# W_down in one run of 36 rows a partition, its operand turned on VectorE: a change at the end of a transfer-bound decode kernel

## The chip, the cores and the metric

The kernel runs on one core of one Trainium2 chip. The metric is device microseconds of one execution; lower is better. Executions are repeated, and medians are given with their range. A profiled execution gives the trace; its span, from the first to the last instruction, is about 1.3 us shorter than the time.

## The reference, cut to what matters

One decode step for four sequences: attention over the last 4,096 cached positions of 16 key and value heads, a residual, a layer norm, then a gated feed-forward block and a second residual. The change touches only the last matrix product and what feeds it.

```python
h  = x + attention(layernorm(x), k_cache, v_cache, wq, wo)      # cut
n  = layernorm(h)
gate = n @ W_gate                    # [4, 576] @ [576, 4608]
up   = n @ W_up
hh   = relu(gate) * up               # [4, 4608]
h2   = h + hh @ W_down               # [4, 4608] @ [4608, 576]
```

The operands are bfloat16. W_down is 4608 x 576 x 2 B = 5.31 MB; keys and values together are 134 MB.

## The kernel before: the parts that matter

All loads are issued from SyncE in one queue, far ahead of their use. On chip (in SBUF, the engines' working memory; PSUM is the memory in which TensorE adds up its products) hh lies as four blocks of 32 partitions (only the first four of each block are real sequences), 1,152 columns a block: block j holds features 1152 j to 1152 j + 1151.

```python
# loads, in queue order: ... wo, W_gate, W_up, then W_down block by block
for j in range(4):
    for r0, r1 in ((0, 9),) if j < 3 else ((0, 3), (3, 6), (6, 8), (8, 9)):
        place(("wd", j, r0), ...,   # rows r0..r1 of the 9 that each partition holds of block j
              dma_start(out=arena[...],
                        in_=B_W_down[j*1152:(j+1)*1152].rearrange("(p r) n -> p (r n)", p=128)[:, r0*D:r1*D]))
...
# operand: nine 128x128 transposes on TensorE, three copies out of PSUM
for r in range(9):
    transpose(out=bankb[...], in_=hv[:, r, :], identity=ident_b)
copy(hhT[:, 0:512]); copy(hhT[:, 512:1024]); copy(hhT[:, 1024:1152])
...
# the product: 36 rows, two column groups of 288, in PSUM partitions 0-31 and 32-63
for j in range(4):
    for r in range(9):
        for n in range(2):
            matmul(bank[n][32*n:32*n+32, 0:288], lhsT=hhT[:, r*128+32*j:][:, 0:32], rhs=wv[:, r, 288*n:288*(n+1)])
vector.tensor_copy(out_sb[0:32],  bank[0][0:32, 0:288])      # then SyncE sends 4 rows
scalar.copy(out_sb[32:64], bank[1][32:64, 0:288])            # then ScalarE sends 4 rows
```

## Time and profile before

| what | value |
|---|---|
| time | 377.98 us (377.96 to 378.03, 3 runs) |
| packets of the load queue | 98.8% of the time of 16 DMA engines |
| VectorE, TensorE, ScalarE busy | 60%, 55%, 14% |
| W_up's last piece in use | 361.94 us |
| last row of W_down in use | 374.39 us |
| end of the span | 376.6 us |

The prediction below shows the page's transfer rows, the chain and the timeline of the end. Two more lines matter. The first, of the page, counts the packets of all queues by size. The view after it cuts the end into stretches; its columns are the stretch, its length, the busy time and the number of instructions of each engine, the clock granted to TensorE as a part of full speed, the busy share of the DMA engines, and GB/s.

```profile
DMA packets 6802, 159.74 MB, mean 424 GB/s; under 512 B 764, under 2 KB 904, under 8 KB 1672
```

### The profile page before, as it was taken

What the parts mean: (1) busy time and instruction counts of PE and PEld (TensorE: products, weight loads), DVE (VectorE), ACT (ScalarE), POOL (GpSimd) and SP (SyncE); (2) the same over time, 40 slices, a digit from 0 to 9 for tenths busy, and PEclk for the clock granted to TensorE, in tenths of its full rate; (3) what the DMA queues carried; (4) which work ended last, traced back from release to release, by engine and by line L of the source; (5) the groups of instructions that cost most, each with busy time, mean ns of one, the idle gap of its engine ahead of it and who ended that gap; (6) DMA issues with size and microseconds to landing.
All of it is one profiled execution on the core that took longest, in us unless ns stands there. A gap on an engine that the chain in (4) does not pass through costs nothing.

```text
span 376.6 us, 2562 instructions
## 1 busy us (share of the span) xinstructions
PE 208.8 (55%) x1456; PEld 37.6 (10%) x703; DVE 226.2 (60%) x164; ACT 54.3 (14%) x85; POOL 10.5 (3%) x29
## 2 busy tenths in 40 slices
PE   0304443249919191749282845664655687886674
PEld 0000000001101010001010100100000001002422
DVE  3078888779292959584847777665659423333220
ACT  3193000301000114010101140101010401112010
POOL 8200000000000000000000000000000000000000
PEclk9955888859968797687788796989696968998699
DMA  8999999999999999999999999999999999999996
GB/s 335 446 439 428 416 442 439 428 418 442 437 425 421 439 440 421 421 442 442 425 419 439 442 428 418 438 439 428 425 435 439 423 425 439 422 431 425 437 413 260
DMA packets 6802, 159.74 MB, mean 424 GB/s; under 512 B 764, under 2 KB 904, under 8 KB 1672
## 3 DMA queue, kind: packets, MB, share of 16 engines
q1 hardware_dynamic: 6776, 159.59, 98.8%
q8 instruction: 8, 0.13, 0.1%
q10 hardware_dynamic: 16, 0.01, 0.0%
q14 instruction: 2, 0.02, 0.0%
HBM read 159.58 MB, written 0.00 MB: 424 GB/s over the span
## 4 chain that ended last, share of the span: by engine, by line
DMA 56%; PE 21%; DVE 20%; issue 1%; SPq 1%; ACT 0%
DMA sb_arena<-in_A_k_cache_dram 48%; DVE sb_arena L425 16%; PE psb L34 13%; DMA sb_arena<-in_B_W_down_dram 9%; PE psb L449 4%; PE psb L510 3%; DVE sb_o_tmp L523 1%; DVE sb_pp L488 1%; PE psb L476 1%; SPq L284 0%; DVE sb_pp L471 0%; DVE sb_hx L454 0%; ACT sb_pp L468 0%; PE psb L705 0%; DVE sb_out_sb L708 0%
## 5 line engine op out<-in xcount | busy, mean ns | idle before, releaser
L425 DVE STREAM_TRANSPOSE sb_arena<-sb_arena 128x8192 f32<-128x8192 f32 (+1 forms) x19 | 139.9, 7365 | 66.4 <-DMA sb_arena<-in_A_k_cache_dram 66.4
L449 PE MATMUL psb<-sb_arena 128*32 128x512 bf16 x256 | 44.5, 640 | 118.8 <-DVE sb_arena L425 118.8
L34 PE MATMUL psb<-sb_arena,sb_pp 128*128 128x512 bf16 x382 | 107.3, 389 | 2.9 <-issue 2.8
L510 PE MATMUL psb<-sb_arena,sb_pp 128*128 128x512 bf16 x115 | 44.8, 389 | 8.9 <-DVE sb_o_tmp L523 8.9
L34 PE MATMUL psb<-sb_arena 128*32 128x512 bf16 x256 | 45.4, 645 | 0.0
L520 ACT COPY sb_o_tmp<-psb 32x512 f32<-32x512 f32 x32 | 18.5, 577 | 181.7 <-PE psb L34 181.4
L523 DVE TENSOR_TENSOR sb_o_tmp<-psb,sb_fm 32x512 f32<-32x512 f32 x32 | 21.7, 678 | 18.6 <-PE psb L34 18.1
L449 PEld LDWEIGHTS psb<-sb_arena 128*32 128x32 bf16 x256 | 9.7, 117 | 162.0 <-DVE sb_arena L425 131.8
L510 PEld LDWEIGHTS psb<-sb_arena,sb_pp 128*128 128x128 bf16 x128 | 12.8, 100 | 115.7 <-issue 115.7
L527 DVE TENSOR_REDUCE sb_o_sel<-sb_o_tmp 128x128 f32<-128x512 f32 x16 | 17.7, 1107 | 0.5
L468 ACT ACTIVATE sb_pp<-psb,sb_hx 128x1024 bf16<-128x1024 f32 x4 | 4.5, 1113 | 79.4 <-DVE sb_hx L465 79.4
L488 DVE TENSOR_TENSOR sb_pp<-psb,sb_m 128x1024 bf16<-128x1024 f32 x8 | 9.3, 1206 | 4.6 <-PE psb L476 4.6
L483 ACT ACTIVATE sb_pp<-psb,sb_m 128x512 bf16<-128x512 f32 x16 | 9.8, 698 | 14.6 <-PE psb L476 14.6
L526 DVE TENSOR_TENSOR sb_o_tmp<-sb_o_tmp,sb_fm 64x512 f32<-64x512 f32 x16 | 11.0, 689 | 0.5
L416 ACT COPY sb_arena<-sb_q_keep 32x256 bf16<-32x256 bf16 x8 | 9.7, 1448 | 0.1
L402 DVE CAST sb_pp<-psb 128x512 bf16<-128x512 f32 x1 | 2.4, 2425 | 10.1 <-PE psb L382 10.1
L471 DVE STREAM_TRANSPOSE sb_pp<-sb_pp 128x1024 bf16<-128x1024 bf16 x4 | 5.0, 1245 | 5.1 <-ACT sb_pp L468 5.1
L476 PE MATMUL psb<-sb_pp,sb_to_v 128*32 128x256 bf16 x64 | 4.3, 400 | 6.2 <-DVE sb_pp L471 6.2
L705 PE MATMUL psb<-sb_arena,sb_pp 128*32 128x288 bf16 x72 | 5.4, 288 | 3.8 <-DMA sb_arena<-in_B_W_down_dram 3.8
L708 DVE CAST sb_out_sb<-psb 32x288 bf16<-32x288 f32 x1 | 0.4, 446 | 9.7 <-PE psb L705 9.7
L454 DVE TENSOR_REDUCE sb_hx<-psb 128x1 f32<-128x1024 f32 x4 | 4.9, 1225 | 2.3 <-PE psb L34 2.3
L34 PE MATMUL psb<-sb_arena,sb_hnT 128*32 128x384 bf16 x80 | 6.3, 394 | 0.0
(123 smaller groups left out, 80.4 us busy)
## 6 DMA issues: line engine op xcount, KB each, us to landing
sb_arena<-in_A_k_cache_dram SPq DMA_DIRECT2D x16, 4096.0 KB, 26.1
sb_arena<-in_A_v_cache_dram SPq DMA_DIRECT2D x16, 4096.0 KB, 28.6
sb_arena<-in_A_wo_dram SPq DMA_DIRECT2D x1, 4608.0 KB, 25.3
sb_arena<-in_B_W_gate_dram SPq DMA_DIRECT2D x1, 4608.0 KB, 26.9
sb_arena<-in_A_wq_dram SPq DMA_DIRECT2D x1, 4096.0 KB, 13.1
sb_arena<-in_B_W_down_dram SPq DMA_DIRECT2D x3, 1296.0 KB, 30.9
sb_arena<-in_B_W_up_dram SPq DMA_DIRECT2D x1, 3456.0 KB, 27.8
sb_arena<-in_B_W_up_dram SPq DMA_DIRECT2D x1, 1152.0 KB, 30.3
```

Source lines behind the costliest of these rows:

```text
L34: return e.add_instruction(mybir.InstMatmult(name=e.bass.get_next_instruction_name(), engine=mybir.EngineType.PE, ins=[e.lower_ap(rhs), e. ...
L416: act("QW", lambda e, i=i, q=q: e.copy(out=bass.AP(tensor=arena, offset=32 * i * AW + 2 * i + q, ap=[[AW, 32], [512, 16], [136, 4], [32, 4]]),
L425: dve(("TRA", g), lambda e: e.transpose(out=dst, in_=src), [("L", "K", g)] if lo == 0 else [])
L449: fn = lambda e, out_=out_, lhsT=lhsT, rhs=rhs, start=start, stop=stop: e.matmul(out_, lhsT=lhsT, rhs=rhs, start=start, stop=stop, skip_gr ...
L476: pe(("RM", b, n // 2), lambda e, n=n, i=i: e.matmul(bank[6 if n < 2 else 0][32 * i:32 * i + 32, n % 2 * 256:n % 2 * 256 + 256], lhsT=to_v ...
L483: act(("EV", b, 0), lambda e, a=a: e.activation(out=bass.AP(tensor=pp, offset=2 * a, ap=[[PPW, 128], [8, 2], [32, 128], [1, 2]]), in_=bank ...
L488: dve(("EV", b, 1), lambda e, n=n: e.tensor_tensor(out=bass.AP(tensor=pp, offset=16 + 8 * n, ap=[[PPW, 128], [32, 128], [2, 4], [1, 2]]), ...
L510: fn = lambda e, lhsT=lhsT, rhs=rhs, k=k, j=j: e.matmul(bank[2 + j], lhsT=lhsT, rhs=rhs, start=(k == 0), stop=(k == 7), skip_group_check=True)
L520: act(("OSC", g), lambda e, j=j: e.copy(out=o_tmp[32 * j:32 * j + 32, 0:512], in_=bank[2 + j][32 * j:32 * j + 32, :]), [("PV", g), ("OSEL" ...
L523: dve(("OSD", g), lambda e, j=j: e.tensor_tensor(out=ot(32 * j, 32), in0=bank[2 + j][32 * j:32 * j + 32, :].rearrange("p (t d) -> p t d", ...
L526: dve(("OS", g), lambda e: e.tensor_tensor(out=ot(64, 64), in0=ot(64, 64), in1=fmb(64, 64), op=ALU.mult), [("OSC", g)])
L527: dve(("OSEL", g), lambda e: e.tensor_reduce(out=o_sel[:, qd, b, :], in_=o_tmp[:, 0:512].rearrange("p (t d) -> p d t", d=DH), axis=AX.X, o ...
```

## The change

The intent, as the diff shows it: longer runs in memory and fewer transfers for W_down, no detour of the operand over TensorE and PSUM, and output columns split so that ScalarE copies more of the output than VectorE. If partition p holds rows 36 p to 36 p + 35, all of its W_down is one run of 41,472 B, and the operand that row r needs is hh with each 32x32 block turned, which VectorE does in SBUF (two instructions, 1.23 us each in the trace of the changed kernel). Both belong together: the layout of W_down decides how hh must be turned.

```diff
-        for j in range(4):
-            for r0, r1 in ((0, 9),) if j < 3 else ((0, 3), (3, 6), (6, 8), (8, 9)):
-                place(("wd", j, r0), ...)
+        WD_ROWS = (0, 15, 25, 32, 35, 36)
+        for r0, r1 in zip(WD_ROWS, WD_ROWS[1:]):
+            place(("wd", r0), wd_off + r0 * D, (r1 - r0) * D, ("DOWN", 1),
+                  ... in_=B_W_down.rearrange("(p r) n -> p (r n)", p=128)[:, r0 * D:r1 * D]))
 ...
-        for r in range(9): pe(transpose(...))      # and the three copies HC0, HC1, HC2
+        for i in range(2):
+            dve(("HHT", i), lambda e, i=i: e.transpose(
+                out=hhT[:, 576 * i:576 * i + 576].rearrange("p (r q) -> p r q", q=32),
+                in_=bass.AP(tensor=pp, offset=3712 + 18 * i, ap=[[PPW, 128], [1, 18], [36, 32]])), ...)
+        ncol = ((0, 224), (224, 576))
 ...                                                 # both matmul groups, evictions and outputs use ncol
```

More of the change, by code (lines that the diff above doesn't have):

```diff
@@ L190, in bass_sequential_preLN__sliding_block_cached__glu_gated_reglu__decode_kernel @@
         tmp5 = sb("tmp5", [128, DC, B], FP32)
-        out_sb = sb("out_sb", [128, 288], BF16)
+        out_sb = sb("out_sb", [128, 352], BF16)
         pT = pp[:, 0:4096]
@@ L277, in bass_sequential_preLN__sliding_block_cached__glu_gated_reglu__decode_kernel @@
                 off += n
-        WDJ = 9 * D
-        wd_off = []
-        for j in range(4):
-            wd_off.append(off)
-            for r0, r1 in ((0, 9),) if j < 3 else ((0, 3), (3, 6), (6, 8), (8, 9)):
-                place(("wd", j, r0), off + r0 * D, (r1 - r0) * D, ("DOWN", 1),
-                      lambda e, off=off, j=j, r0=r0, r1=r1: e.dma_start(
-                          out=arena[:, off + r0 * D:off + r1 * D],
-                          in_=B_W_down[j * 1152:(j + 1) * 1152, :].rearrange("(p r) n -> p (r n)", p=128)[:, r0 * D:r1 * D]))
-            off += WDJ
+        WD_ROWS = (0, 15, 25, 32, 35, 36)
+        wd_off = off
+        for r0, r1 in zip(WD_ROWS, WD_ROWS[1:]):
+            place(("wd", r0), wd_off + r0 * D, (r1 - r0) * D, ("DOWN", 1),
+                  lambda e, r0=r0, r1=r1: e.dma_start(
+                      out=arena[:, wd_off + r0 * D:wd_off + r1 * D],
+                      in_=B_W_down.rearrange("(p r) n -> p (r n)", p=128)[:, r0 * D:r1 * D]))
         pool("c_eps", lambda e: e.memset(eps_c[:, :], EPS))
@@ L678, in bass_sequential_preLN__sliding_block_cached__glu_gated_reglu__decode_kernel @@
                 [("G", m), ("GUM", 1, m)])
-        hv = hh.rearrange("p (q r) -> p r q", r=9)
-        for r in range(9):
-            dst = bankb[(6, 5, 7)[r // 4]][:, r % 4 * 128:r % 4 * 128 + 128]
-            pe(("HTR", r), lambda e, r=r, dst=dst: e.transpose(out=dst, in_=hv[:, r, :], identity=ident_b[:, :]),
-               [("HH", m) for m in range(3)] + ["s1", "h1"] if r == 0 else [])
-        dve("HC0", lambda e: e.tensor_copy(out=hhT[:, 0:512], in_=bankb[6][:, 0:512]), [("HTR", 3)])
-        act("HC1", lambda e: e.copy(out=hhT[:, 512:1024], in_=bankb[5][:, 0:512]), [("HTR", 7)])
@@ L686, in bass_sequential_preLN__sliding_block_cached__glu_gated_reglu__decode_kernel, with down @@
-        dve("HC2", lambda e: e.tensor_copy(out=hhT[:, 1024:1152], in_=bankb[7][:, 0:128]), [("HTR", 8)])
+        for i in range(2):
+            dve(("HHT", i), lambda e, i=i: e.transpose(
+                out=hhT[:, 576 * i:576 * i + 576].rearrange("p (r q) -> p r q", q=32),
+                in_=bass.AP(tensor=pp, offset=3712 + 18 * i, ap=[[PPW, 128], [1, 18], [36, 32]])), [("HH", m) for m in range(3)])
+        ncol = ((0, 224), (224, 576))
+        def down(n, lhsT, w, start, stop):
+            lo, hi = ncol[n]
+            return lambda e: e.matmul(bank[n][32 * n:32 * n + 32, 0:hi - lo], lhsT=lhsT, rhs=w[:, lo:hi], start=start, stop=stop,
+                                      skip_group_check=True)
@@ L689, in bass_sequential_preLN__sliding_block_cached__glu_gated_reglu__decode_kernel @@
         for n in range(2):
-            pe(None, lambda e, n=n: e.matmul(bank[n][32 * n:32 * n + 32, 0:288], lhsT=sel4[:, :], rhs=part[:, 288 * n:288 * (n + 1)],
-                                             start=True, stop=False, skip_group_check=True), [("G", 1)])
+            pe(None, down(n, sel4[:, :], part, True, False), [("G", 1)])
         for n in range(2):
-            pe(None, lambda e, n=n: e.matmul(bank[n][32 * n:32 * n + 32, 0:288], lhsT=ident_b[0:B, 0:32], rhs=x_bf[:, 288 * n:288 * (n + 1)],
-                                             start=False, stop=False, skip_group_check=True))
@@ L695, in bass_sequential_preLN__sliding_block_cached__glu_gated_reglu__decode_kernel @@
-        for j in range(4):
-            wv = arena[:, wd_off[j]:wd_off[j] + WDJ].rearrange("p (r n) -> p r n", n=D)
-            for r in range(9):
-                for n in range(2):
-                    deps = []
-                    if n == 0:
-                        if r == 0 or (j == 3 and r in (3, 6, 8)):
-                            deps.append(("L", "wd", j, r))
-                        if j == 0 and r in (0, 4, 8):
-                            deps.append(f"HC{r // 4}")
-                    pe(("DOWN", n), lambda e, j=j, r=r, n=n, wv=wv: e.matmul(
-                        bank[n][32 * n:32 * n + 32, 0:288], lhsT=hhT[:, r * 128 + 32 * j:r * 128 + 32 * j + 32],
-                        rhs=wv[:, r, 288 * n:288 * (n + 1)], start=False, stop=(j == 3 and r == 8), skip_group_check=True), deps)
@@ L708, in bass_sequential_preLN__sliding_block_cached__glu_gated_reglu__decode_kernel @@
-        dve("OUT0", lambda e: e.tensor_copy(out=out_sb[0:32, :], in_=bank[0][0:32, 0:288]), [("DOWN", 0)])
-        act("OUT1", lambda e: e.copy(out=out_sb[32:64, :], in_=bank[1][32:64, 0:288]), [("DOWN", 1)])
+            pe(None, down(n, ident_b[0:B, 0:32], x_bf[:, :], False, False))
+        for r in range(36):
+            for n in range(2):
+                deps = []
+                if n == 0:
+                    if r in WD_ROWS:
+                        deps.append(("L", "wd", r))
+                    if r % 18 == 0:
+                        deps.append(("HHT", r // 18))
+                pe(("DOWN", n), down(n, hhT[:, 32 * r:32 * r + 32], arena[:, wd_off + r * D:wd_off + r * D + D], False, r == 35), deps)
@@ L710, in bass_sequential_preLN__sliding_block_cached__glu_gated_reglu__decode_kernel @@
+        dve("OUT0", lambda e: e.tensor_copy(out=out_sb[0:32, 0:224], in_=bank[0][0:32, 0:224]), [("DOWN", 0)])
+        act("OUT1", lambda e: e.copy(out=out_sb[32:64, 0:352], in_=bank[1][32:64, 0:352]), [("DOWN", 1)])
         orow = out.rearrange("b s d -> (b s) d")
         for n in range(2):
-            P.dma(("sync", "scalar")[n], ("O", n), lambda e, n=n: e.dma_start(
-                out=orow[:, 288 * n:288 * n + 288], in_=out_sb[32 * n:32 * n + 4, :]),
+            lo, hi = ncol[n]
+            P.dma(("sync", "scalar")[n], ("O", n), lambda e, n=n, lo=lo, hi=hi: e.dma_start(
+                out=orow[:, lo:hi], in_=out_sb[32 * n:32 * n + 4, 0:hi - lo]),
```

## The prediction

Where it sizes the arrivals, "this" is a fixed cost of each transfer; "a bf16 128x1024 one" is a transpose on VectorE. The terms of its sum, -0.08 + 0 + 0 + 0.10 - 0.03, came to -0.01 us. But for the first the trace gives 0.06 us, the step to 0.08 was my own, and with 0.06 the sum is +0.01.

> **What bounds the kernel now.** I read the page's slices (part 2) first, then its DMA part (3), then the chain that ended last, cut to the last 17 us, and then the timeline of the same stretch.
>
> ```profile
> DMA  8999999999999999999999999999999999999996
> GB/s 335 446 439 428 416 442 439 428 418 442 437 425 421 439 440 421 421 442 442 425 419 439 442 428 418 438 439 428 425 435 439 423 425 439 422 431 425 437 413 260
> q1 hardware_dynamic: 6776, 159.59, 98.8%
> ```
>
> The DMA row stands at 9 in every slice but the first and the last: one queue carries 159.59 MB and its packets fill 98.8% of the time of 16 DMA engines. Nothing else is near that (VectorE 60%, TensorE 55% on the page). So the kernel ends when the last byte has come in plus whatever must follow that byte. The chain says which transfer that is and what follows:
>
> ```profile
> 341.69 32.31 DMA sb_arena<-in_B_W_down_dram
> 374.00 0.04 issue
> 374.04 0.70 PE psb L705 x6
> 374.74 0.43 DVE sb_out_sb L708
> ```
>
> The last W_down transfers were issued by 341.7 us and came in at 374.0 us: 32 us in the queue behind earlier loads, not 32 us of work of their own. After them come six small matmuls, one eviction and the output transfer, some 2.5 us to the span's end at 376.6. The timeline of that stretch shows what each engine does while W_down arrives:
>
> ```profile
> 362.41 1.49 DVE L676 TENSOR_TENSOR sb_pp<-psb,sb_pp 128x384 bf16<-128x384 f32 x3 [7.59 <-PE psb L667]
> 363.95 0.76 PE L682 MATMUL psb<-sb_ident_b,sb_pp 128*128 128x128 bf16 x9 [1.34 <-DVE sb_pp L676]
> ...
> 365.47 1.28 PE L705 MATMUL psb<-sb_arena,sb_pp 128*32 128x288 bf16 x18
> ...
> 368.13 1.28 PE L705 MATMUL psb<-sb_arena,sb_pp 128*32 128x288 bf16 x18 [1.37 <-DMA sb_arena<-in_B_W_down_dram]
> ...
> 371.23 1.65 PE L705 MATMUL psb<-sb_arena,sb_pp 128*32 128x288 bf16 x24 [1.82 <-DMA sb_arena<-in_B_W_down_dram]
> ...
> 374.39 0.10 PEld L705 LDWEIGHTS psb<-sb_arena,sb_pp 128*32 128x32 bf16 x2 [0.24 <-DMA sb_arena<-in_B_W_down_dram]
> 374.73 0.45 DVE L708 CAST sb_out_sb<-psb 32x288 bf16<-32x288 f32 x1 [9.73 <-PE psb L705]
> 374.76 0.39 ACT L709 CAST sb_out_sb<-psb 32x288 bf16<-32x288 f32 x1 [9.49 <-PE psb L705]
> 375.18 0.28 ACTq L712 DMA_DIRECT2D out_dram<-sb_out_sb  x1
> 375.20 0.34 SPq L712 DMA_DIRECT2D out_dram<-sb_out_sb  x1
> ```
>
> Every burst of W_down matmuls after the first waits for a DMA (the brackets: 1.37, 1.82, 0.24 us of idle time). TensorE keeps up, so only what follows 374.39, the arrival of the last row, is exposed.
>
> [...]The trace lets me size this: successive arrivals at 368.12 and 371.22 are 3.10 us apart for 1,327,104 B (82,944 B an engine), those at 373.33 and 374.04 are 0.71 us apart for 294,912 B (18,432 B an engine). The difference is 64,512 B in 2.39 us, 27.0 B/ns an engine, and what is left is 0.71 - 18,432/27.0 ns = 0.03 us a transfer: a fixed cost is there, and tiny. [...]here a bf16 128x1024 one takes 1245 ns (page, L471), about 1.2 ns a column with its fixed part[...]. [...]18 matmuls of 288 columns in 1.28 us, one alone 0.29, are (1.28 - 0.29)/17 = 0.058 us apart, so the two column groups of a row overlap and a row takes about 0.117 us.
>
> **The change part by part.**
>
> 1. *Seven W_down transfers become five, with the same bytes* (36 rows of 1,152 B a partition, 5.31 MB). Longest runs go from 10,368 B to 17,280 B; the last piece is still one row, 1,152 B a partition. At 0.03 us fixed a transfer, two fewer save 2 x 0.03 = 0.06 us of the queue[...]. I take **-0.08 us** on the path, and expect the last row at about 374.3.
>
> 2. *The first transfer is issued later.* It is now 15 rows long and reaches into the slot that the last value tile leaves, so it must wait for that tile's matmuls (they end at 339.9) where its predecessor went out at 332.1. At 339.9 the queue still holds the gate and up weights: the last up piece is used at 361.94. So 22 us of queue lie ahead of it: **0 us**. Two issues of some 0.4 us fewer on SyncE likewise cost or gain nothing.
>
> 3. *The operand hh is turned on VectorE.* Nine TensorE transposes and three PSUM copies go (363.95 to about 365.3, with the copies), two VectorE transposes of 128x576 come. Scaled from 1245 ns for 1024 columns: 576/1024 x 1245 = 0.70 us, say 0.8 with the fixed part not shrinking; two follow the products at 363.9, so the operand is whole at about 365.5. The source is strided now (36 elements between columns); if that doubled it, 367.1. When is it needed? The first piece holds 15 rows and lands later than before's 9-row piece: 361.9 + 15 x 1,152 x 8 / 27.0 ns = 361.9 + 5.12 + 0.03 = 367.05. So all of this lies beside the DMA: **0 us**.
>
> 4. *Columns 224 and 352 in place of 288 and 288.* A row's pace is now that of the wider group: 352/288 x 0.117 = 0.143 us. Pieces should land at 367.05, 370.5 (10 rows, 3.44 later), 372.9 (7 rows, 2.42), 374.0 (3 rows, 1.05) and 374.3 (one row, about 0.36). TensorE needs 2.15, 1.43, 1.00 and 0.43 us for the first four: done at 369.2, 371.9, 373.9, 374.43. Only the fourth comes within the reach of the last arrival: the last row may start some 0.1 us after it landed, **+0.05 to +0.1 us**. Its wide matmul takes 64 columns more, 64/288 x 0.117 = **+0.03 us**.
>
> 5. *The evictions.* VectorE's 0.45 us for 288 columns falls to about 0.38 (a 128x128 copy at 0.29 and a 128x288 one at 0.46 give 1.06 ns a column), and it may begin a little earlier. ScalarE's 0.39 rises by 64 x 0.83 ns (0.577 for 512 columns against 0.39 for 288) to 0.44. Before, the two transfers went out at 375.18 and 375.20 and SyncE's issue took longer (0.34 against 0.28), so its path was last by 0.08. Now ScalarE's is last, with 0.05 added to a path that had 0.08 to spare: **-0.03 us**.
>
> Sum: -0.08 + 0 + 0 + 0.10 + (-0.03) is about 0.0. With the uncertainty of the last two terms I put the change at -0.05 us: **377.9 us** from 377.98.
>
> **The rivals.** (a) *The transfer is hidden anyway, and the tail alone moves*: this is my main line. (b) *The new layout streams faster*: longer runs bring the last 12.5 us of the queue to its best slices, 442 GB/s where 5.31 MB in 12.5 us are 425. That would save 0.5 us, 377.5. Against it: the fixed part measured above leaves only 0.2 us in all to be had on these seven transfers. (c) *TensorE or VectorE becomes the bound in the tail*: if strided reading made the transposes four times as long (3 us each), the operand would come at 370, and with 36 rows at 0.143 us, 5.1 us, TensorE would end at 375.1, 0.6 us late: 378.5. Against it: the large strided transposes on the float32 keys run at 8712 ns for 8192 columns, 1.06 ns each[...]. (d) *The queue runs dry because the first W_down transfer is issued late*: it would need 22 us less in the queue, excluded by the arrival times. (e) *Partitions now lie 41,472 B apart in memory, and reading goes slower*: nothing in the trace speaks for it, as the up weights, also slices of longer rows, come at full rate (437 GB/s in their slice). A loss of 5% on 12.5 us would be 0.6 us.
>
> **Range and chances.** The three runs of before lie within 0.07 us of each other, so noise is small; the rivals reach from -0.5 to +0.6 us. The range is **377.4 to 378.4**. A 2% change is 7.6 us; the whole of W_down takes 12.5 us to come in and cannot shrink by half. So **within 2% at 0.98**, 0.01 each for faster and slower.
>
> **What would show it right or wrong.** In the changed kernel the DMA row is still 9 throughout; W_down matmuls wait for DMA at about 367, 370.5 and 372.9; the two VectorE transposes take 0.7 to 0.8 us each and end before the first piece lands; the last matmul waits little or nothing for DMA, since the row before it is only just done; ScalarE's eviction ends after VectorE's. The prediction is wrong if TensorE's first W_down burst waits for VectorE, if the last arrival moves by more than 0.3 us, or if the output transfers take a different time to finish than before.

## More of the kernel before

```profile
364.00:366.00 2.00, 2.00 (x25) 1.25 (x27) 0.56 (x2) 0.58 (x1) 0.00 (x0) 1.00 1.03 430
366.00:368.00 2.00, 0.75 (x14) 0.38 (x8) 0.00 (x0) 0.00 (x0) 0.00 (x0) 1.00 1.02 430
368.00:370.00 2.00, 1.28 (x18) 0.82 (x18) 0.00 (x0) 0.00 (x0) 0.00 (x0) 1.00 0.97 408
370.00:372.00 2.00, 0.77 (x14) 0.64 (x16) 0.00 (x0) 0.00 (x0) 0.00 (x0) 1.00 0.98 397
```

Here TensorE (first busy column) has work in every stretch, never for the whole of the last three, and the clock column says 1.00.

## The result, and the profile after

The changed kernel takes **377.92 us** (377.72 to 378.18, 6 runs), against 377.97 us (377.88 to 378.09, 6 runs) for the kernel before on the same chip. The ratio is 0.9998 with a 95% interval of 0.9985 to 1.0011: the same. Ratios here and below are the mean time of one kernel's fast runs over that of the other's of the same rounds, so not quite the ratio of the medians quoted beside them.

The page's transfer lines of the changed kernel, to be set against those of before:

```profile
GB/s 335 446 435 432 413 446 446 425 411 446 444 421 414 443 444 421 414 446 446 421 413 446 446 418 421 438 446 418 425 439 446 413 432 435 430 423 426 437 414 263
DMA packets 6514, 159.74 MB, mean 424 GB/s; under 512 B 736, under 2 KB 872, under 8 KB 1512
q1 hardware_dynamic: 6488, 159.58, 98.8%
```

There are 288 packets fewer, and the queue is as full and as fast as it was. Next, the chain that ended last, from 355 us, and the timeline of the end:

```profile
338.23 34.60 DMA sb_arena<-in_B_W_down_dram
372.83 0.04 issue
372.88 1.86 PE psb L685 x19
...
374.76 0.44 ACT sb_out_sb L702
```

```profile
361.91 0.35 PE L664 MATMUL psb<-sb_arena,sb_hnT 128*32 128x384 bf16 x4 [1.14 <-DMA sb_arena<-in_B_W_up_dram]
...
362.38 1.49 DVE L673 TENSOR_TENSOR sb_pp<-psb,sb_pp 128x384 bf16<-128x384 f32 x3 [8.97 <-PE psb L664]
...
363.89 2.39 DVE L677 STREAM_TRANSPOSE sb_pp<-sb_pp 128x576 bf16<-128x576 bf16 x2
...
367.04 7.68 PE L685 MATMUL psb<-sb_arena,sb_pp 128*32 128x224 bf16 x72 [3.63 <-DMA sb_arena<-in_B_W_down_dram]
...
372.88 0.86 PEld L685 LDWEIGHTS psb<-sb_arena,sb_pp 128*32 128x32 bf16 x14 [0.48 <-DMA sb_arena<-in_B_W_down_dram]
373.95 0.45 PEld L685 LDWEIGHTS psb<-sb_arena,sb_pp 128*32 128x32 bf16 x8 [0.21 <-DMA sb_arena<-in_B_W_down_dram]
374.62 0.38 DVE L701 CAST sb_out_sb<-psb 32x224 bf16<-32x224 f32 x1 [8.34 <-PE psb L685]
374.76 0.44 ACT L702 CAST sb_out_sb<-psb 32x352 bf16<-32x352 f32 x1 [15.56 <-PE psb L685]
375.03 0.34 SPq L706 DMA_DIRECT2D out_dram<-sb_out_sb  x1
375.24 0.27 ACTq L706 DMA_DIRECT2D out_dram<-sb_out_sb  x1
```

The end is where it was: ScalarE's eviction starts at 374.76 in both. What leads up to it is quite different. TensorE waits 3.63 us for the first piece, and then its 72 matmuls run as one piece of 7.68 us, where before they came in bursts with waits between. The stretches show the clock beside it (the same columns as above):

```profile
364.00:366.00 2.00, 0.00 (x0) 0.00 (x0) 2.00 (x2) 0.00 (x0) 0.00 (x0) 0.50 0.96 409
366.00:368.00 2.00, 0.96 (x10) 0.89 (x12) 0.29 (x1) 0.00 (x0) 0.00 (x0) 0.50 0.96 409
368.00:370.00 2.00, 2.00 (x20) 1.25 (x17) 0.00 (x0) 0.00 (x0) 0.00 (x0) 0.50 0.98 416
370.00:372.00 2.00, 2.00 (x24) 1.28 (x22) 0.00 (x0) 0.00 (x0) 0.00 (x0) 0.81 0.99 412
```

With its transposes gone and the first piece 15 rows long, TensorE has nothing to do from 363.4 to 367.0 us, a gap of 3.63 us. By the clock records of the trace, which the page only sums up, its clock is granted at half from 363.94 to 370.77 us. The matmuls of 352 columns started 0.293 us apart within that time, and 0.149 after it wherever they had no wait.

It is tempting to say that this gap brought the clock down. The traces do not agree: the clock fell only 0.53 us after TensorE's last matmul, and it fell in before352 and before_drop6 too, where no gap from 361 us to the fall was above 1.34 us.

What differs is how long it stayed down. The clock records of before and of the changed kernel (39 and 40 of them) change only at intervals that are multiples of 3.41 us. In before352 and before_drop6 the clock was at half for one such interval (364.33 to 367.74 and 364.06 to 367.47); TensorE worked through all of it, and the clock came back at its end. In the changed kernel it was at half for two, 6.83 us: TensorE had work for only 0.31 us of the first (363.94 to 367.35) and for the whole of the second. So in these traces the clock stayed down, into the work on W_down, where TensorE had the gap; warm, below, tests whether the gap is the cause. How little work makes it fall can't be read from them: it fell after an interval with 1.75 us of matmuls in the changed kernel, and stayed up after one with 1.59 us in the kernel before (368.69 to 372.10).

So the question was this. The time is unchanged, as forecast, but is it so because all the changed work is hidden, or because a slower TensorE eats up what a faster queue gains?

### The profile page after: what moved, and what is told of

It is laid out like the page before. It is cut to its first block, busy times and chain, and to the rows that moved or that the text cites. A ratio compares the mean times of both kernels' runs of the same rounds, so it can differ in the third digit from the quotient of the medians.

```text
span 376.5 us, 2541 instructions
## 1 busy us (share of the span) xinstructions
PE 209.2 (56%) x1447; PEld 39.2 (10%) x694; DVE 227.6 (60%) x164; ACT 53.8 (14%) x84; POOL 10.7 (3%) x29
## 4 chain that ended last, share of the span: by engine, by line
DMA 62%; DVE 18%; PE 18%; SPq 1%; issue 1%; ACT 0%
DMA sb_arena<-in_A_k_cache_dram 53%; DVE sb_arena L422 16%; PE psb L34 11%; DMA sb_arena<-in_B_W_down_dram 9%; PE psb L446 4%; PE psb L507 2%; DVE sb_o_tmp L520 1%; DVE sb_pp L485 1%; PE psb L685 0%; SPq L242 0%; PE psb L473 0%; SPq L282 0%; ACT sb_out_sb L702 0%; SPq L255 0%; SPq L251 0%
## 5 line engine op out<-in xcount | busy, mean ns | idle before, releaser
L446 PE MATMUL psb<-sb_arena 128*32 128x512 bf16 x256 | 42.5, 629 | 119.1 <-DVE sb_arena L422 119.0
L34 PE MATMUL psb<-sb_arena,sb_pp 128*128 128x512 bf16 x382 | 105.2, 383 | 2.7 <-issue 2.6
L507 PE MATMUL psb<-sb_arena,sb_pp 128*128 128x512 bf16 x115 | 44.1, 383 | 8.9 <-DVE sb_o_tmp L520 8.9
L34 PE MATMUL psb<-sb_arena 128*32 128x512 bf16 x256 | 44.2, 649 | 0.0
L685 PE MATMUL psb<-sb_arena,sb_pp 128*32 128x352 bf16 (+1 forms) x72 | 7.6, 349 | 3.7 <-DMA sb_arena<-in_B_W_down_dram 3.6
L673 DVE TENSOR_TENSOR sb_pp<-psb,sb_pp 128x384 bf16<-128x384 f32 x3 | 1.5, 551 | 9.0 <-PE psb L664 9.0
L379 PE MATMUL psb<-sb_arena,sb_xnT 128*32 128x512 bf16 x16 | 2.6, 628 | 7.2 <-DMA sb_arena<-in_A_wq_dram 7.2
L664 PE MATMUL psb<-sb_arena,sb_hnT 128*32 128x384 bf16 x40 | 4.2, 405 | 3.9 <-DVE sb_hnT L645 2.0
```

Of the source, the lines that this page charges most:

```text
L34: return e.add_instruction(mybir.InstMatmult(name=e.bass.get_next_instruction_name(), engine=mybir.EngineType.PE, ins=[e.lower_ap(rhs), e. ...
L446: fn = lambda e, out_=out_, lhsT=lhsT, rhs=rhs, start=start, stop=stop: e.matmul(out_, lhsT=lhsT, rhs=rhs, start=start, stop=stop, skip_gr ...
L507: fn = lambda e, lhsT=lhsT, rhs=rhs, k=k, j=j: e.matmul(bank[2 + j], lhsT=lhsT, rhs=rhs, start=(k == 0), stop=(k == 7), skip_group_check=True)
L685: return lambda e: e.matmul(bank[n][32 * n:32 * n + 32, 0:hi - lo], lhsT=lhsT, rhs=w[:, lo:hi], start=start, stop=stop, skip_group_check=True)
```

## The experiments

Time, and from each profile the moment at which W_up's last piece is in use, the start of ScalarE's last eviction, and the difference. The difference takes out what happens before W_down's turn in the queue, which moves by up to 0.3 us from run to run. Each is of one execution, so a difference of a few hundredths says little.

| kernel | time us, median (range) | ratio to before, 95% interval | W_up in use | eviction | difference |
|---|---|---|---|---|---|
| before | 377.98 | | 361.94 | 374.76 | 12.82 |
| changed | 377.92 (377.72 to 378.18) | 0.9998 (0.9985 to 1.0011) | 361.91 | 374.76 | 12.85 |
| cols288 | 377.94 (377.87 to 378.18) | 0.9997 (0.9983 to 1.0011) | 362.00 | 374.78 | 12.78 |
| warm | 377.94 (377.70 to 378.11) | 0.9995 (0.9983 to 1.0008) | 361.89 | 374.73 | 12.84 |
| warm288 | 378.86 (377.96 to 379.14) | 1.0017 (1.0003 to 1.0031) | 362.06 | 374.88 | 12.82 |
| before352 | 377.83 (377.69 to 378.08) | 0.9993 (0.9981 to 1.0006) | 361.85 | 374.72 | 12.87 |
| pieces7 | 377.88 (377.81 to 377.97) | 0.9993 (0.9978 to 1.0008) | 361.93 | 374.97 | 13.04 |
| turn_twice | 378.40 (378.32 to 379.25) | 1.0012 (0.9995 to 1.0028) | 361.84 | 375.90 | 14.06 |
| turn_flat | 377.93 (one run) | none | 362.11 | 374.93 | 12.82 |
| before_drop6 | 376.07 (376.04 to 376.24) | 0.9946 (0.9930 to 0.9963) | 361.98 | 372.98 | 11.00 |
| after_drop6 | 377.90 (377.05 to 378.30) | 0.9990 (0.9972 to 1.0009) | 362.14 | 374.67 | 12.53 |
| after_drop6_warm | 376.12 (376.03 to 377.32) | 0.9961 (0.9947 to 0.9976) | 362.04 | 373.05 | 11.01 |
| after_drop6_288 | 376.97 (376.53 to 377.50) | 0.9974 (0.9961 to 0.9987) | 362.02 | 374.18 | 12.16 |
| warm7_288 | 377.91 (377.83 to 379.17) | 1.0010 (0.9998 to 1.0023) | 362.02 | 374.77 | 12.75 |

The profiled run of turn_twice is the longest of its four, 379.25.

### One part at a time: columns and clock

cols288 puts the columns back to 288 and 288.

```diff
-        ncol = ((0, 224), (224, 576))
+        ncol = ((0, 288), (288, 576))
```

> The changed kernel with 288 and 288 columns again. Theory A (TensorE slips behind the arrivals because its clock was granted at half from 364 to 370 us and because the 352-column group sets the pace of a row): a row goes from 0.29 us to 0.24 us at half clock and from 0.147 to 0.12 at full clock, the backlog at 372.9 us is smaller, the last matmuls end 0.1 to 0.2 us sooner: time 377.7 to 377.85. Rival B (the last arrival alone sets the end, the column split only moves the evictions by 0.05 us): 377.9 to 378.0, unchanged.

Its 0.12 us is the pace of a row in the kernel before, where rows of 288 and 288 columns started 0.122 us apart at full clock; the 0.24 is an estimate, twice that.

warm gives TensorE something to do in the gap, 14 matmuls; nothing reads what they write. warm288 does both.

```diff
+        for _ in range(14):
+            pe(None, lambda e: e.matmul(bank[7][0:32, :], lhsT=hnT[:, 0, :], rhs=arena[:, gu_off[(0, 0)]:gu_off[(0, 0)] + 512],
+                                        start=True, stop=True, skip_group_check=True))
         for r in range(36):
```

> The changed kernel with 14 matmuls of 512 columns into an unused bank, placed in the 3.6 us in which TensorE waits for the first W_down piece; the result stays right. Theory A: the clock stays at 1.0 through 364 to 370 us, the W_down matmuls wait for the DMA before each of the five pieces, the last arrival is again in the chain; time 0.1 us below the changed kernel, about 377.8. Rival B: clock changed or not, time unchanged within 0.05 us at 377.9.

> Both at once. Theory A: this is the fastest, last matmul right behind the last arrival (within 0.4 us), which is 0.1 to 0.2 us earlier than in the kernel before: 377.7 to 377.8. Rival B: 377.9 to 378.0.

before352 is the kernel before with 224 and 352 columns in the product, evictions and outputs, and nothing else.

> The kernel before with 224 and 352 columns alone. Both theories: within 0.1 us of 377.97, since TensorE waits for every W_down piece there; a row takes 0.143 us in place of 0.117, ScalarE's eviction 0.44 us in place of 0.39 and ends last, VectorE's 0.38 in place of 0.45. If the time moves by over 0.2 us, the split matters by itself and both are wrong.

The clock did what was expected. In warm's stretches it stands at 1.00 throughout, and TensorE waits for its pieces again:

```profile
367.02 2.42 PE L685 MATMUL psb<-sb_arena,sb_pp 128*32 128x224 bf16 x30 [0.50 <-DMA sb_arena<-in_B_W_down_dram]
370.42 1.67 PE L685 MATMUL psb<-sb_arena,sb_pp 128*32 128x224 bf16 x20 [0.98 <-DMA sb_arena<-in_B_W_down_dram]
372.86 1.84 PE L685 MATMUL psb<-sb_arena,sb_pp 128*32 128x224 bf16 x22 [0.77 <-DMA sb_arena<-in_B_W_down_dram]
```

The time did not: 377.94, and a difference of 12.84 us against 12.85. Theory A's gain of 0.1 us is not there. The columns alone, in either kernel, move the difference by 0.05 to 0.07 us and the time by nothing that can be told from noise. The difference stops at the eviction, and so misses that the split gains a little after it: from the start of ScalarE's eviction to the end of the span there are 1.70 to 1.74 us in all eight kernels with 224 and 352 columns, 1.82 to 1.84 in all six with 288 and 288. In full, then, the changed kernel's slower TensorE costs no time: it has caught up by 372.88, when the piece that ends the chain comes in (its weight loads wait 0.48 us for that piece in the timeline above; its last matmul before it ends at about 372.76, so it is a near thing). warm288 was about a microsecond longer in four of its five executions; more of this below.

### Longer runs

pieces7 cuts the new layout into the old sizes.

```diff
-        WD_ROWS = (0, 15, 25, 32, 35, 36)
+        WD_ROWS = (0, 9, 18, 27, 30, 33, 35, 36)
```

> The changed kernel with W_down cut into 9, 9, 9, 3, 3, 2 and 1 rows, the sizes of before. If my 0.03 us a transfer is right, the last row arrives 0.06 to 0.16 us later after the up weights than in the changed kernel; the first piece is in at 365.0 and TensorE then waits for VectorE until 366.3. Time within 0.1 us of 377.92 either way; a rival by which the longer runs matter (442 against 425 GB/s) expects 0.5 us more, 378.4.

The packet records of the traces, which the page only sums up, have the moment of each transfer's last completion. From the end of W_up to the end of W_down there are 12.59 us in the kernel before, 12.55 in before352 and 12.54 in pieces7, all with seven transfers. There are 12.43 us in the changed kernel, and 12.43 to 12.46 in cols288, warm and warm288, all with five. So two transfers fewer are worth about 0.12 us of the queue, and the layout by itself, pieces7 against before, 0.05 at most; that it is no loss answers rival (e) of the prediction too. The two transfers are 288 packets, 18 an engine, and the runs don't tell a cost of the packet from one of the transfer. The time of pieces7 is 377.88: the longer runs are not worth the 0.5 us of the rival, and 0.12 us cannot be seen in the time. Its difference of 13.04 us in the table is of its profiled execution, in which the clock stood at half until 373 us and TensorE ran behind the pieces from 371.2 us on.

### How much room is left beside the queue

An unchanged time says that the work is hidden, not by how much. Taking bytes away shows it: if the queue alone sets the end, six rows of 36 fewer must bring it 2.05 us forward (an estimate, at 432 GB/s). In before_drop6 and after_drop6 these rows are not loaded and loaded rows are used twice, so TensorE's work stays whole. The result is wrong. The comparison with the reference passed all the same, so it is too coarse to see this and says nothing here; by itself it does not prove the changed kernel right either. The edit of after_drop6 (before_drop6 drops the same number of rows in the old layout):

```diff
-        WD_ROWS = (0, 15, 25, 32, 35, 36)
+        WD_ROWS = (0, 15, 25, 26, 29, 30)
...
-        for r in range(36):
+        for r, wr in zip(range(36), [*range(15), *range(6), *range(15, 30)]):   # wr: the row of weights
```

> The kernel before with 30 of the 36 rows of W_down loaded (wrong result on purpose): six rows reuse weights of the first piece, and TensorE still runs all 72 matmuls. Theory A (the end is the arrival of the last bytes plus a fixed tail): 6 x 1,152 B x 128 partitions less at 432 GB/s is 2.05 us less: 375.9. Rival B (TensorE or the operand's path stands as close behind as the queue): less than 1 us gained, 377.0 to 377.9.

> The changed kernel with 30 of 36 rows loaded, in the same way. Theory A: 2.05 us less as well: 375.85. Theory C (the change has used up the slack beside the queue: TensorE cannot start before 367.0 and its clock is granted at half until about 370): it would end some 0.5 us earlier than the changed kernel only, 377.2 to 377.5, with TensorE and not a DMA in the chain. So the two kernels with rows dropped would differ by over a microsecond although the full ones do not differ.

The kernel before gains 1.93 us (376.07 against 378.00). The changed kernel gains nothing to speak of, less even than theory C expected: 377.90 against 377.92, with executions from 377.05 to 378.30. The chains of the two, before_drop6 first:

```profile
337.74 33.48 DMA sb_arena<-in_B_W_down_dram
...
371.27 1.69 PE psb L705 x24
372.96 0.43 DVE sb_out_sb L708
```

```profile
337.48 29.73 DMA sb_arena<-in_B_W_down_dram
...
367.25 7.40 PE psb L685 x43
...
374.67 0.44 ACT sb_out_sb L702
```

In before_drop6 a piece of W_down at 371.27 is still what TensorE follows. In after_drop6 the last DMA in the chain is the *first* piece, at 367.2; from there TensorE works for 7.40 us without waiting for anything, and the later pieces lie in SBUF unused: the DMA engines carry nothing after 372 us, TensorE works until 374.65. So the change has used up nearly 2 us of room beside the queue (1.83 by the medians, 376.07 against 377.90), which the full kernel does not show. The clock alone does not tell the two apart, since it was at half in before_drop6 as well, but there only until 367.47, against 371.03 in after_drop6:

```profile
364.00:366.00 2.00, 2.00 (x13) 1.09 (x13) 0.65 (x2) 0.58 (x1) 0.00 (x0) 0.51 0.99 420
366.00:368.00 2.00, 2.00 (x22) 1.10 (x22) 0.00 (x0) 0.00 (x0) 0.00 (x0) 0.63 1.00 425
```

Two more kernels say what used the room.

> 30 of 36 rows loaded, as after_drop6, with 7 matmuls of 512 columns into an unused bank while TensorE waits for the first piece (about 1.5 us at full clock, 3.0 us at half). If the lost slack is the clock[...], the clock stays at 1.0, a row takes 0.147 us, TensorE waits for pieces again, and the time falls from 377.9 to about 376.1, close to before_drop6. If it is the late start at 367 and the wider group, at most 0.5 us is gained: 377.4 to 377.9.

The 1.5 and 3.0 us in it are estimates: seven times the 0.216 us from one 512-column matmul to the next at full clock in the kernel before, and twice that. In the trace the seven took 1.68 us, at full clock.

> after_drop6 with 288 and 288 columns. If the wider group alone used up the slack: 376.1. If the clock did most: at half clock a row takes 0.24 in place of 0.293 us, at full 0.12 in place of 0.147; 36 rows that took 7.4 us take 6.1 to 6.5, so 1.0 us is gained: 376.7 to 377.1, still with TensorE in the chain.

after_drop6_warm, with seven matmuls in the gap, takes 376.12 us: all of the room is back, and the difference is 11.01 us, before_drop6's 11.00. Its clock stays at 1.00 from 362 us on, and a DMA at 370.6 is in its chain again:

```profile
337.68 32.88 DMA sb_arena<-in_B_W_down_dram
...
370.60 2.43 PE psb L685 x26
```

In the traces of all four kernels with matmuls in the gap (warm, warm288, after_drop6_warm, warm7_288) the clock did not fall there. One of the four executions of after_drop6_warm took 377.32 all the same; it was not traced.

after_drop6_288 takes 376.97: half of it is back, with TensorE in the chain from the first piece on. Its 72 matmuls took 6.96 us where after_drop6's took 7.38, though its clock was at half longer, until 372.04. So the idle gap, by way of the clock that stays at half into the work on W_down, is enough to explain the lost room; that TensorE starts at 367 and with the wider group does not cost it by itself, as after_drop6_warm has both. Why after_drop6's executions spread over 1.25 us can't be settled without a trace of each. As above, the clock of before and of the changed kernel changes only at multiples of 3.41 us from its other changes, but the moments differ from execution to execution: the half-clock time of the changed kernel and its variants without matmuls in the gap is 6.83 us in all seven (in pieces7 with waits of only 1.89 and 0.74 us), and it begins anywhere from 363.94 (changed) and 365.21 (after_drop6_288) to 366.30 (turn_twice). The later it begins, the more of the work on W_down falls into it. That this makes the spread of after_drop6 is likely but not shown.

### The operand

> The changed kernel with a contiguous source for the two VectorE transposes (wrong result on purpose). They took 1.195 us each with a source of 36 elements' stride, where I had scaled 0.70 from 1245 ns for 1024 columns. If the stride costs the rest, they take 0.70 to 0.80 here; if not, 1.2. The time stays at 377.9 either way, as the operand waits for the DMA.

> The changed kernel with the two VectorE transposes done twice, 2.39 us more. The operand was whole at 366.3 and first used at 367.0, so 0.76 us of it is hidden and TensorE starts at about 368.7. Theory A (TensorE catches up beside the queue): 377.9 to 378.1. Theory C (slack used up): TensorE ends later, 0.3 to 1.5 us longer, 378.2 to 379.4, with VectorE in the chain.

turn_flat reads `hh[:, 576 * i:576 * i + 576]` in place of the strided pattern, which gives a wrong result. One line of the instruction view of the changed kernel, then the same of turn_flat (shortest, median and longest, in ns):

```profile
L677 DVE STREAM_TRANSPOSE sb_pp<-sb_pp x2: 1210/1233/1256, 363.9 to 365.1; 128x576 bf16<-128x576 bf16 x2
```

```profile
L677 DVE STREAM_TRANSPOSE sb_pp<-sb_pp x2: 736/757/778, 364.1 to 364.8; 128x576 bf16<-128x576 bf16 x2
```

The stride costs 1233 - 757 = 476 ns each, or 0.83 ns a column. The time is 377.93, as expected: the operand is early in both.

turn_twice repeats both transposes ahead of the ones that count. Three of its four executions took 378.32 to 378.43, above all six of the changed kernel, though those are of other rounds and the interval of its ratio includes 1. My expectation had the start of TensorE wrong: it began at 367.65, not 368.7, because the first 18 rows need only the first of the two.

```profile
366.25 2.39 DVE L681 STREAM_TRANSPOSE sb_pp<-sb_pp 128x576 bf16<-128x576 bf16 x2
367.65 8.21 PE L689 MATMUL psb<-sb_arena,sb_pp 128*32 128x224 bf16 x72 [4.31 <-DVE sb_pp L681]
```

A start 0.6 us later brought VectorE into the chain of the profiled execution, and the median rose by about 0.45 us. This fits the missing room, seen from the other side, but at 0.1% it is not shown. In the profiled execution, the longest, the clock stood at half until 373 us, where the changed kernel's was back at 370.77; this may be its extra 0.8 us.

### A candidate, and what stays open

warm7_288 is the full kernel with 288 columns and seven matmuls in the gap.

> The full load with 288 columns and 7 matmuls in the wait, where warm288 had 14 and was 1 us longer in four of five runs. If those runs came from the 14 matmuls themselves (6 us at half clock, past the first arrival), this one has none of them and lies at 377.7 to 377.95. If they came from elsewhere, slow ones show here too, 378.9. It is also the candidate to beat both; by more than 0.3 us only if the arrivals are not the bound.

The 6 us in it is an estimate, 14 times the 0.216 us above, doubled; at full clock, in warm, the 14 took 3.20 us. No trace has them at half clock.

Its difference of 12.75 us is the smallest of all full kernels, by 0.07 us against before, and its median is 377.91. Four executions took 377.83 to 377.95 and two took 379.05 and 379.17. So 14 matmuls are not needed for the long ones of warm288: the expectation that named them falls. Nor is either part enough by what was run: warm (14 matmuls, 224 and 352 columns) and cols288 (288 columns, no matmuls) had none in five each. Executions about 1 us longer also occurred in the kernel before (378.97 and 378.93, 2 of 32 over all rounds). The mean clocks of the long ones are those of ordinary ones too: 0.801 to 0.815 in warm288's, 0.796 in an ordinary one of before. Their traces were not taken, so where that microsecond arises, and whether matmuls in the gap make it more frequent, stays open. No version here beats the kernel before by an amount that can be told from noise.

## Why the prediction was right

Forecast 377.9 us (377.4 to 378.4), measured 377.92. That the forecast change of -0.05 us came out as -0.05 is luck: the runs of the changed kernel spread over 0.46 us, and the terms of the prediction add up to -0.01, not -0.05. By its steps:

1. **Five transfers, -0.08 us.** Right in kind, a little small: the packet records give -0.12.
2. **The later issue costs nothing.** Right. The transfers were issued from 337.4 us on (I had put it at 339.9), and W_down followed W_up in the queue with no gap: its first packets start at 359.62, W_up's last end at 361.42.
3. **The operand is hidden.** Right for the time; its size was wrong. I took 0.8 us a transpose and measured 1.23, because I held the stride to be free on the strength of the float32 key transposes. That was a misreading: by the kernel's code (`turn_k`) those read their source in order and write in runs of two adjacent words, so they say nothing of a source that jumps at every element. The operand was whole at 366.3, 0.76 us ahead of the first piece. turn_flat shows what the stride costs a bf16 source that steps 72 B: 2.14 ns a column, against 1.31 contiguous, each with the fixed part.
4. **Columns: the wider group sets a row's pace, +0.10 us.** The mechanism is right at full clock: warm's rows took (2.42 - 0.31)/14 = 0.15 us, warm288's (2.02 - 0.31)/14 = 0.12. At the end, the wide matmul of the last row did not wait for its own arrival: the chain enters TensorE at 372.88 and stays there, and that matmul starts at 374.41, 0.10 us after the narrow one of its row, as forecast. The columns alone cost 0.05 us in before352 by the difference.
5. **Evictions.** Right: VectorE's took 0.38 us, ScalarE's 0.44, and ScalarE's eviction ended last (375.20 against 375.00). The gain was mis-sized: 0.11 us from the start of the eviction to the end of the span (above), where I had 0.03. What makes up the rest was not tested; the output transfers end a little sooner (1.22 us from the last issue to the end of the span, against 1.39), which was one of the prediction's own signs of being wrong.

What the working missed is what removing TensorE's work from the gap does to its clock, and so to the room beside the queue. It forecast waits at 367, 370.5 and 372.9. TensorE's matmuls waited for long only at 367.0; warm, at full clock, has all three (367.02, 370.42, 372.86). Of its other signs of being right, only the 0.7 to 0.8 us a transpose failed. Rival (c), TensorE becoming the bound in the tail, was argued against by the speed of transposes; it came to within about 0.1 us (372.76 against 372.88) by another way, the clock. Here it cost nothing, since the queue still ended later.

Shown: the end follows the queue in the kernel before (before_drop6), and in the changed kernel TensorE stands right behind it (after_drop6) because of the gap (after_drop6_warm). Argued only: that the moment at which the half-clock time begins makes the spread of after_drop6, and that turn_twice's 0.45 us is the missing room.

## What to carry to other kernels

Here transfers set the end, and moving work off one engine changed nothing in the time (377.92 us against 377.97), but it used up 1.8 us of room that the next improvement may need; drop some bytes (with a wrong result) to measure how much is left. Before removing work from TensorE, look at the gap it leaves: here the clock stood at half for the first 3.7 us of the work that followed 3.6 us without any, and with seven matmuls in that time (after_drop6_warm) the clock stayed at 1.00 and the 1.8 us were back. And look at the clock of more than one execution before you say what brought it down. Last, a time that agrees with the forecast is no proof of the steps: the clock column of the stretches told more than the time.
